# Vector products whose rows come out on their own partitions, and 32x32 transpositions for the way to columns

## The chip, the core and the metric

The kernel runs on one core of one Trainium2 chip. The metric is the device time of one execution in microseconds. Each kernel is run several times and the median is compared.

Engines are called as the profile calls them: PE (TensorE; PEld is its weight load), DVE (VectorE), ACT (ScalarE), POOL (GpSimd) and SP (SyncE). PE reads SBUF and writes PSUM. DVE and ACT read and write both.

## What is computed

One token passes through four layers, A B A B, and then back. A is attention with one query over the last 4096 positions of a cache, B is an MLP. Both A layers share their weights, and so do both B layers. The results are the output and the gradients of the input, of both caches and of all weights.

```
x = x + A(layernorm(x));  x = x + B(layernorm(x))      # twice
A(x):  q = x @ wq (1024 -> 32 heads x 128, 4 kv heads)
       p = softmax(q k^T * 128**-0.5) over the last 4096 of 32768 positions
       return (p v) @ wo                               # 4096 -> 1024
B(x):  h = x @ w1 + b1                                 # 1024 -> 3584
       return (h * tanh(softplus(h))) @ w2             # 3584 -> 1024
out, grads = value and vjp with grad_out               # all tensors bf16
```

The gradient of a cache is zero outside the last 4096 positions, so 56 MB of zeros are written. The gradients of the weights are outer products of two vectors per layer pair.

## The kernel before

All vectors are held as columns: element 128t + p on partition p, column t (for the 3584 and 4096 long ones of the MLP and of wo, element 512c + 4p + k in column 4c + k). The order of instructions on each engine is written out by hand.

**Loads.** SP loads weights in chunks of 1 MB into a ring of eight slots (class `Ring`, L71 issues). `want` lists them in order; `pump` issues as long as a slot is free; `release` frees a slot and pumps. W1, the first MLP matrix, stays in SBUF in the tile `W1`. After the way back through layer 0's MLP its place is used anew: `ring.lend(lent)` gives three slots in it to the ring, and `ROWS`, `rt`, `rf`, `RT` and `TWIN` lie in the rest of it.

**Zeros.** `zeros(n)` takes n of 56 jobs of 1 MB each and issues them on POOL from the zeroed tile `zt` (L272). The calls are spread over the program by hand, most of them behind a value that has to be there first (L267, `pz`). `zt` holds a weight chunk until POOL zeroes it in `last_da` (L808).

**Products forward.** Where a matrix is used in its natural layout, a product with a vector has two forms.

- The column form makes a 128x128 block the weights and one column the moving operand, so each block costs a weight load and a matmul of one column, and the result is a column at once. Layer 0's MLP uses it: L680 for the first product, `mlp_out` (L744) for the second, into `y_ps`. So does `dn_b0`, the way back through layer 0's first MLP product, over blocks `STAY` to 27 of W1 (`mv`, L500, into `TP`). By then these blocks have been turned in place, and only the first `STAY` = 4 blocks of each row are in natural layout; for them DVE computes eight dot products (`rowdot`, L458, into `dnp`).
- The row form (`row_mm`, L351) repeats the vector over 32 weight columns and streams the matrix, so the result is a row in PSUM, on 32 partitions alike. Four such matmuls stand side by side in four column groups of the array (`tile_position=(0, 32 * j)`).

The row form is used for layer 1's wo product and second MLP product (`rows_by_two`: even rows into groups 0 and 1, odd rows into groups 2 and 3, two halves of 512) and for layer 1's first MLP product (seven pieces of 512 in the banks `SC[0]` and `SC[1]`). The way from the rows to columns goes over DVE or ACT copies to SBUF and fp32 matmuls with the selection matrices `sel2` or `sel4` (L365 and L367 in `two_to_cols`, L689 and L692 in `mlp_fwd`). `residual` (L416) adds the old x; L705 adds the bias.

**The way back.** `rows_chunk` goes through a chunk's four rows of blocks: the first `nr` of them as dot products on DVE, the others turned by PE (`turn_pe`, L481), copied to SBUF by DVE or ACT (`evac`, L313 and L316, by a running estimate of both loads) and then multiplied in the column form (L500). `later` holds these products back a few units, and a chunk is released behind its last product. `do1`, `dp1`, `dq1` and `dn1` are hooks that are called after each chunk of the last attention's way back. `do1(4)` turns the output y to columns and adds x3.

**Rows for the outer products.** The weight gradients need the vectors as rows. `put_by` writes four of them to DRAM early on (L826) and `take_back` (L830) brings them into `ROWS`; `rowize` (L1025, L1028, L1030) and `rowize_f` (L868, L870, L872) turn others by PE, copy them by ACT and move them into `ROWS` by SP's queue. All are called within `dn_b0`, after its rows 2 and 4, besides `rowize(GA)` in `do1(0)` and `rowize(DQC)` in `dq1`.

**The end.** After g0 PE computes the outer products (L1066, L1117), DVE and ACT copy them to SBUF, and SP stores them.

Of the kernel before, what the change touches and what calls it, by code (L numbers as in the profile page):

```python
# [93 lines left out]
def kernel(  # L94
# [97 lines left out]
    nc.vector.memset(spread[:], 0.0)  # L192
    sel4 = sb([P, 4], FP32, "sel4")
    nc.vector.memset(sel4[:], 0.0)
    sel2 = sb([P, 2], FP32, "sel2")
    nc.vector.memset(sel2[:], 0.0)
    for j in range(4):
        nc.vector.memset(sel4[32 * j:32 * j + 1, j:j + 1], 1.0)
        nc.vector.memset(sel2[32 * j:32 * j + 1, j % 2:j % 2 + 1], 1.0)
    quarter = sb([P, 4], FP32, "quarter")  # L200
# [147 lines left out]

    def row_mm(bank, j, stat, mov, first, last):

        nc.tensor.matmul(bank[32 * j:32 * j + 32, :], lhsT=stat.to_broadcast([P, 32]), rhs=mov, start=first, stop=last,  # L351
                         skip_group_check=True, tile_position=(0, 32 * j))

    def rows_by_two(bank, ch, c, n, vec):

        for tt in range(4):
            k = 4 * c + tt
            for s in range(2):
                row_mm(bank, 2 * (k % 2) + s, vec(k), ch[:, tt, 512 * s:512 * s + 512], k < 2, k >= n - 2)

    def two_to_cols(bank, buf, out):

        ov = out.rearrange("p (s i) -> p i s", s=2)
        for h in range(2):
            nc.vector.tensor_copy(buf[:, 256 * h:256 * h + 256], bank[:, 256 * h:256 * h + 256])  # L365
            for i in (2 * h, 2 * h + 1):
                nc.tensor.matmul(ov[:, i, :], lhsT=buf[:, i * P:(i + 1) * P], rhs=sel2[:], start=True, stop=True,  # L367
                                 skip_group_check=True)

# [51 lines left out]

    def ln_bwd(part, n32, rstd, g, name, beside=None):

        st = tmp([P, 2], FP32, "bst")
        dn = tmp([P, TD], FP32, "dn")
        t2 = tmp([P, TD], FP32, "t2")
        if part is None:
            nc.vector.tensor_scalar(out=dn[:], in0=TP[:, 0:TD], scalar1=1.0, scalar2=0.0, op0=ALU.mult, op1=ALU.add,
                                    accum_out=st[:, 0:1])
        else:  # L430
            nc.vector.scalar_tensor_tensor(out=dn[:], in0=TP[:, 0:TD], scalar=1.0, in1=part[:], op0=ALU.mult, op1=ALU.add,
                                           accum_out=st[:, 0:1])
        nc.vector.scalar_tensor_tensor(out=t2[:], in0=dn[:], scalar=1.0, in1=n32[:], op0=ALU.mult, op1=ALU.mult,
                                       accum_out=st[:, 1:2])
        if beside is not None:
            beside(0)
        nc.tensor.matmul(TP[:, 128:130], lhsT=onesD[:], rhs=st[:], start=True, stop=True)
        if beside is not None:
            beside(1)
        ab = tmp([P, 2], FP32, "ab")  # L440
        nc.vector.tensor_copy(ab[:], TP[:, 128:130])
        nc.vector.scalar_tensor_tensor(out=t2[:], in0=n32[:], scalar=ab[:, 1:2], in1=dn[:], op0=ALU.mult,
                                       op1=ALU.subtract)
        nc.vector.tensor_scalar(out=t2[:], in0=t2[:], scalar1=ab[:, 0:1], scalar2=rstd[:, 0:1], op0=ALU.add,
                                op1=ALU.mult)
        gn = sb([P, TD], FP32, f"g_{name}")
        nc.vector.tensor_sub(gn[:], g[:], t2[:])
        return gn
# [82 lines left out]
    def attn_fwd(l, x, st, first, wo_hook, q_hook=None):  # L531
# [88 lines left out]
        for c in range(8):  # L620
            ch = ring.get(("o", l, c))
            if not first:
                rows_by_two(YR, ch, c, HQ, lambda h: OC[:, h, l:l + 1])
                wo_hook(c)
                continue
            for tt in range(4):
                h = 4 * c + tt
                for dd in range(TD):
                    nc.tensor.matmul(y_ps[:, dd:dd + 1], lhsT=ch[:, tt, dd * P:(dd + 1) * P], rhs=OC[:, h, l:l + 1],
                                     start=(h == 0 and dd == 0), stop=(h == HQ - 1), skip_group_check=True)  # L630
            ring.release(("o", l, c))
            wo_hook(c)
        if not first:
            two_to_cols(YR, small, y_ps)
        xn, stn = residual(y_ps, x, name)
# [36 lines left out]
    def mlp_fwd(l, x, st, mid):  # L672
# [9 lines left out]
        else:  # L682
            for t in range(TD):
                for c in range(7):
                    row_mm(SC[c // 4], c % 4, NB[:, t, l:l + 1], W1[:, t, 512 * c:512 * c + 512], t == 0, t == TD - 1)
            hv = [h_ps[:, 0:16].rearrange("p (j k) -> p k j", k=4), h_ps[:, 16:28].rearrange("p (j k) -> p k j", k=4)]
            for b, (buf, copy) in enumerate(((small, nc.vector.tensor_copy), (mlp_t, nc.scalar.copy))):
                n = 32 * (4, 3)[b]
                copy(buf[0:n, :], SC[b][0:n, :])  # L689
                bv = buf[0:n, :].rearrange("p (m k) -> p k m", k=4)  # L690
                for k in range(4):
                    nc.tensor.matmul(hv[b][:, k, :], lhsT=bv[:, k, :], rhs=sel4[0:n, 0:n // 32], start=True, stop=True,  # L692
                                     skip_group_check=True)

# [9 lines left out]
        V = nc.vector  # L704
        V.tensor_tensor(out=h[:], in0=h_ps, in1=b1c[:], op=ALU.add)  # L705

# [31 lines left out]
        return dict(n32=n32, rstd=rstd, deriv=deriv, act_late=act_late)  # L738

    def mlp_out(l, ch, c, y_ps):  # L740
        for tt in range(4):
            fb = 4 * c + tt
            for dd in range(TD):
                nc.tensor.matmul(y_ps[:, dd:dd + 1], lhsT=ch[:, tt, dd * P:(dd + 1) * P], rhs=AC[:, fb, l:l + 1],  # L744
                                 start=(fb == 0 and dd == 0), stop=(fb == TF - 1), skip_group_check=True)


# [42 lines left out]
    mp0 = sB0["deriv"]()  # L790
    y_ps = MV[:, 256:256 + TD]
    for c in range(7):
        mlp_out(0, ring.get(("2", 0, c)), c, y_ps)
        if c == 4:
            da_dots(c)
        if c < 5:
            ring.release(("2", 0, c))
    x2, st2 = residual(y_ps, x1, "B0")

    def last_da(k):  # L800
# [6 lines left out]
        if k:  # L807
            nc.gpsimd.memset(zt[:], 0.0)  # L808

    def wo_hook1(c):  # L810
# [17 lines left out]
    def take_back(name, base, off):  # L828
        r = DR[name][:].rearrange("(n l) p -> l n p", l=2)
        nc.sync.dma_start(ROWS[base:base + 2, off:off + r.shape[1] * P].rearrange("l (n p) -> l n p", p=P), r)  # L830

# [31 lines left out]
    def rowize_f():  # L863
# [7 lines left out]
        for l in range(2):  # L871
            nc.sync.dma_start(ROWS[64 + l:65 + l, NOFF:NOFF + F].rearrange("o (c j) -> o c j", j=512),  # L872
                              rf[:, 512 * l:512 * l + 512])
# [10 lines left out]
    def dn_b0(g):  # L884
        bcast(lambda c: DHC[:, c, 0:1], STAY)
        mv_open()
        for t in range(TD):
            rowdot(W1[:, t, 0:STAY * P], [LB[0][:, 0:512]], 512, dnp[:, t:t + 1], True)
            mv(W1[:, t, STAY * P:], TF - STAY, TP[:, t:t + 1], lambda i: DHC[:, STAY + i, 0:1], True)
            if t == 2:  # L890
                rowize(GB, TD, 96, 0)
                take_back("AC", 96, NOFF)
                take_back("NB", 64, 0)
                take_back("OC", 32, NOFF)
                take_back("NA", 0, 0)
            if t == 4:
                rowize_f()
        return ln_bwd(dnp, sB0["n32"], sB0["rstd"], g, "B0", lambda k: turn_ahead(("o", 3, 0), ((0,), (1, 2))[k]))

# [122 lines left out]
    def rowize(cols, n, base, off):  # L1022
# [6 lines left out]
        for l in range(2):  # L1029
            nc.sync.dma_start(ROWS[base + l:base + l + 1, off:off + n * P].rearrange("o (t p) -> o t p", p=P),  # L1030
                              rt[l:2 * n:2, k, :])
# [112 lines left out]
    da0 = tmp([P, HQ], FP32, "da")  # L1144
    y_ps = MV[:, 384:384 + TD]
    mv_open()
    even()
    bigs.append(SC[1])
    for c in range(7):
        ch = ring.get(("2", 1, c))  # L1150
        rows_by_two(YR, ch, c, TF, lambda fb: AC[:, fb, 1:2])
        flush()
# [11 lines left out]
    g1 = dn_b0(g2)  # L1164
    ring.lend(lent)
    nc.vector.tensor_copy(GA[:, :, 0], g1[:])
# [10 lines left out]
    def do1(c):  # L1177
        if c == 0:
            rowize(GA, TD, 32, 0)
        if c == 3:  # L1180
            todo[1].append(units_rows(32, HQ, out_5))
        if c == 4:
            two_to_cols(YR, RT.rearrange("p a t s -> p (a t s)")[:, 0:1024].bitcast(FP32), y_ps)
            nc.vector.tensor_tensor(out=x4[:], in0=y_ps, in1=x3[:], op=ALU.add)
        if c == 5:
# [29 lines left out]
    g0 = attn_bwd(0, sA0, g1, ("o", 3), ("q", 3), (), dict(do=do1, dp=dp1, dq=dq1, dn=dn1), units_a0)  # L1215
    zeros(3, g0)
    g0b = sb([P, TD], BF16, "g0b")
# [48 lines left out]
```

## Time and profile before

| | |
|---|---|
| runs | 456.04, 454.98, 455.77 us; median 455.77 |
| profiled execution | 455.47 us, span 453.7 us from first to last instruction |
| busy: PE, DVE, ACT, POOL | 327.4, 261.9, 211.4, 38.7 us |
| TensorE clock, mean granted | 0.661 |
| bytes moved | 181.41 MB: 121.84 on the queue of SP, 58.72 on that of POOL |

Busy time of an engine is not the kernel's bound by itself: the stages have different limits. PE's ends are modelled, since matmuls are pipelined. "DMA share" is the mean busy share of the 16 transfer engines, and GB/s what they moved.

### The profile page before, as it was taken

The numbers are of one execution on the slowest core, as the hardware profiler recorded it, in microseconds if no ns is written. First come the engines' busy times: TensorE is split into PE (matmuls) and PEld (weight loads), VectorE is DVE, ScalarE is ACT, GpSimd is POOL, SyncE is SP. The second block draws the span as 40 slices with busy tenths as digits, with TensorE's granted clock in tenths as the row PEclk, the third lists the DMA queues.
The fourth block names the chain that finished last, engine by engine and source line by source line (L and its number), as shares of the span: only waits on it lengthen the run. The fifth ranks groups of instructions, "written<-read, shape, count | busy, mean of one in ns | idle before, by whom it ended". The sixth has DMA issues, their size and how long they took to land. (4 is left out here: it accounts for less than half of the span.)

```text
span 453.7 us, 13076 instructions
## 1 busy us (share of the span) xinstructions
PE 327.4 (72%) x5793; PEld 251.3 (55%) x5793; DVE 261.9 (58%) x523; ACT 211.4 (47%) x246; POOL 38.7 (9%) x86
## 2 busy tenths in 40 slices
PE   3845542556599987998898778888987898889600
PEld 3735542456475686887797547887872222225300
DVE  4504746377451264377366756575386999898600
ACT  2501101011048275577066552364249999999600
POOL 1000000002123121200300101012221000000000
PEclk9955555555559879599679955788585555555555
DMA  8999999989989999999999999999999999999996
GB/s 333 422 423 417 420 418 420 416 313 423 418 363 397 406 407 408 409 392 417 423 422 420 363 387 355 359 411 395 423 413 417 413 416 421 416 422 414 406 408 268
DMA packets 28086, 181.41 MB, mean 400 GB/s; under 512 B 3674, under 2 KB 3702, under 8 KB 9462
## 3 DMA queue, kind: packets, MB, share of 16 engines
q1 hardware_dynamic: 19874, 121.84, 66.2%
q0 software_dynamic: 8064, 58.72, 31.7%
q8 instruction: 45, 0.74, 0.6%
q14 instruction: 11, 0.09, 0.1%
q10 hardware_dynamic: 92, 0.02, 0.0%
HBM read 81.84 MB, written 98.62 MB: 398 GB/s over the span
## 5 line engine op out<-in xcount | busy, mean ns | idle before, releaser
L316 ACT COPY ring<-BIG 128x1024 bf16<-128x1024 bf16 x51 | 50.5, 1015 | 43.6 <-PE BIG L481 21.6
L1066 PE MATMUL wide<-W 2*128 2x512 bf16 x228 | 52.2, 598 | 9.2 <-ACT W L316 2.0
L481 PE MATMUL BIG<-ident_bf,ring 128*128 128x128 bf16 x664 | 55.4, 238 | 3.1 <-issue 1.9
L481 PEld LDWEIGHTS <-ring 128*128 128x128 bf16 x768 | 53.3, 110 | 4.1 <-issue 3.6
L458 DVE CUSTOM_DVE_ANT_0 junk<-ring,SC 128x1024 bf16<-128x1024 bf16 x32 | 38.9, 1215 | 6.3 <-DMA ring<-in_B_w_dram 5.8
L500 PEld LDWEIGHTS <-ring 128*128 128x128 bf16 x864 | 29.6, 97 | 13.5 <-ACT ring L316 6.7
L1066 PEld LDWEIGHTS <-W 2*128 2x128 bf16 x240 | 12.5, 102 | 44.4 <-issue 43.3
L313 DVE CAST ring<-wide 128x1024 bf16<-128x1024 f32 (+1 forms) x29 | 33.8, 1201 | 3.1 <-PE wide L1066 1.1
L316 ACT CAST ring<-wide 128x1024 bf16<-128x1024 f32 (+1 forms) x35 | 32.9, 1011 | 1.3 <-PE wide L1117 0.5
L316 ACT COPY KT<-BIG 128x1024 bf16<-128x1024 bf16 x22 | 21.7, 1013 | 22.8 <-PE BIG L659 20.5
L313 DVE COPY ring<-BIG 128x1024 bf16<-128x1024 bf16 x32 | 21.8, 689 | 17.3 <-PE BIG L481 13.3
L272 POOL DMA_DIRECT2D out_dram<-zt x56 | 29.7, 534 | 21.6 <-DMA out_dram<-zt 20.8
L458 DVE CUSTOM_DVE_ANT_0 junk<-ring,DSX 128x1024 bf16<-128x1024 bf16 x24 | 29.4, 1224 | 0.8
L481 PE MATMUL BIG<-ident_bf,W 128*128 128x128 bf16 x288 | 24.6, 235 | 2.9 <-issue 2.9
L316 ACT COPY W<-BIG 128x1024 bf16<-128x1024 bf16 x21 | 20.8, 1014 | 11.2 <-PE BIG L481 10.7
L543 PE MATMUL MV<-NA,ring 128*128 128x1 bf16 x512 | 15.0, 165 | 13.1 <-DMA ring<-in_A_wq_dram 11.7
L543 PEld LDWEIGHTS <-ring 128*128 128x128 bf16 x512 | 14.6, 103 | 13.8 <-DMA ring<-in_A_wq_dram 12.4
L313 DVE CAST VS<-wide 128x1024 bf16<-128x1024 f32 (+1 forms) x17 | 19.7, 1188 | 3.6 <-PE wide L1066 3.0
L1117 PE MATMUL wide<-W 32*128 32x256 bf16 x128 | 20.9, 402 | 0.9 <-ACT ring L316 0.8
L316 ACT CAST KT<-wide 128x1024 bf16<-128x1024 f32 x20 | 20.4, 1033 | 1.8 <-PE wide L1066 0.9
L481 PEld LDWEIGHTS <-W 128*128 128x128 bf16 x288 | 19.4, 115 | 3.3 <-issue 3.3
L500 PEld LDWEIGHTS <-W 128*128 128x128 bf16 x480 | 16.6, 101 | 3.6 <-issue 2.2
(280 smaller groups left out, 537.9 us busy)
## 6 DMA issues: line engine op xcount, KB each, us to landing
out_dram<-zt POOLq DMA_DIRECT2D x56, 1024.0 KB, 14.3
ring<-in_A_wq_dram SPq DMA_DIRECT2D x24, 1024.0 KB
ring<-in_A_wo_dram SPq DMA_DIRECT2D x14, 1024.0 KB
ring<-in_B_w_dram SPq DMA_DIRECT2D x13, 1024.0 KB
W<-in_A_wo_dram SPq DMA_DIRECT2D x10, 1024.0 KB
W<-in_B_w_dram SPq DMA_DIRECT2D x8, 896.0 KB
out_dram<-ring SPq DMA_DIRECT2D x7, 1024.0 KB
out_dram<-ring SPq DMA_DIRECT2D x13, 512.0 KB
```

The costliest lines, as they stand in the source:

```text
L272: nc.gpsimd.dma_start(dst, zt[:])
L313: nc.vector.tensor_copy(dst, src)
L316: nc.scalar.copy(dst, src)
L458: nc.vector.tensor_tensor_reduce(out=out, in0=a, in1=vec, scale=1.0, scalar=acc if i else 0.0, op0=ALU.mult, op1=ALU.add, accum_out=acc)
L481: nc.tensor.transpose(b[:, i * P:(i + 1) * P], block(w, i) if block else w[:, i * P:(i + 1) * P], ident_bf[:])
L500: nc.tensor.matmul(out, lhsT=w[:, i * P:(i + 1) * P], rhs=rhs_of(i), start=fresh[0], stop=last and i == n - 1, skip_group_check=True)
L543: nc.tensor.matmul(q_ps[:, h:h + 1], lhsT=ch[:, h * P:(h + 1) * P], rhs=NA[:, t, l:l + 1], start=(k == 0 and h == 0), stop=(k == TD - 1), ...
L1066: nc.tensor.matmul(b[:, 512 * i:512 * i + 512], lhsT=R[at:at + 2, lo:lo + P], rhs=R[at:at + 2, ro + 512 * i:ro + 512 * i + 512], start=Tru ...
L1117: nc.tensor.matmul(b[:, k * 256:(k + 1) * 256], lhsT=RT[32 * g:32 * g + 32, a, tp, :], rhs=YS[32 * g:32 * g + 32, :], start=True, stop=Tru ...
```

## The change

1. `rows_by_two` becomes `out_rows`. For each row of blocks, group j now computes those 256 outputs that belong on its own 32 partitions: of each of the eight 128-blocks the elements 32j to 32j + 31. All groups use the same vector column. `two_to_cols` becomes `to_eight`: one DVE transposition of 32x32 blocks over 128x256, whose first column in each block is the column form. The consumer reads it from SBUF with a stride of 32.
2. Layer 1's first MLP product does the same, with 512 columns a group in `SC[0]` and 384 in `SC[1]`; two transpositions and two bias additions follow.
3. Layer 0's second MLP product uses `out_rows` in place of `mlp_out`.
4. `dn_b0` uses the row form over blocks 4 to 27, into `SC[1]`. The eight dot products run in reverse order, and `ring.lend(lent)` comes ahead of `ln_bwd` instead of behind it.
5. `rowize(GB)`, the four `take_back` and `rowize_f` move from `dn_b0` into `do1`, at chunks 0, 1 and 2. All row moves of `rowize`, `rowize_f` and `take_back` are issued by ACT instead of SP.
6. One zero job moves from behind g0 to behind the zeroing of `zt`.
7. `sel2` and `sel4` and their ten memsets go.

```diff
-    def rows_by_two(bank, ch, c, n, vec):
+    def row_mms(bank, n, vec, mov, first, last):
+        for j in range(4):
+            m = mov(j)
+            nc.tensor.matmul(bank[32 * j:32 * j + 32, 0:n].rearrange("p (g a) -> p g a", a=m.shape[-1]),
+                             lhsT=vec.to_broadcast([P, 32]), rhs=m, start=first, stop=last, skip_group_check=True,
+                             tile_position=(0, 32 * j))
+    def out_rows(ch, c, n, vec):
         for tt in range(4):
             k = 4 * c + tt
-            for s in range(2):
-                row_mm(bank, 2 * (k % 2) + s, vec(k), ch[:, tt, 512 * s:512 * s + 512], k < 2, k >= n - 2)
+            row_mms(YR, 256, vec(k), lambda j: ch[:, tt, :].rearrange("p (g q a) -> p q g a", q=4, a=32)[:, j],
+                    k == 0, k == n - 1)
+    def to_eight(bank, buf):
+        nc.vector.transpose(buf[:, 0:256], bank[:, 0:256])
+        return buf[:, 0:256].rearrange("p (g m) -> p g m", m=32)[:, :, 0]
...
             for t in range(TD):
-                for c in range(7):
-                    row_mm(SC[c // 4], c % 4, NB[:, t, l:l + 1], W1[:, t, 512 * c:512 * c + 512], t == 0, t == TD - 1)
+                for b, (c0, c1) in enumerate(((0, 4), (4, 7))):
+                    row_mms(SC[b], 128 * (c1 - c0), NB[:, t, l:l + 1],
+                            lambda j: W1[:, t, :].rearrange("p (c q x) -> p q c x", q=4, x=P)[:, j, c0:c1],
+                            t == 0, t == TD - 1)
...
+            parts = ((0, small, 0, 16), (1, mlp_t, 16, 12))
+            for b, buf, f0, n in parts:
+                V.transpose(buf[:, 0:32 * n].rearrange("p (c k m) -> p c k m", k=4, m=32),
+                            SC[b][:, 0:32 * n].rearrange("p (c a k) -> p c k a", k=4, a=32))
+            for b, buf, f0, n in reversed(parts):
+                V.tensor_tensor(out=h[:, f0:f0 + n], in0=buf[:, 0:32 * n].rearrange("p (f m) -> p f m", m=32)[:, :, 0],
+                                in1=b1c[:, f0:f0 + n], op=ALU.add)
...
-        mlp_out(0, ring.get(("2", 0, c)), c, y_ps)
+        out_rows(ring.get(("2", 0, c)), c, TF, lambda fb: AC[:, fb, 0:1])
...
-        nc.sync.dma_start(ROWS[base:base + 2, off:off + r.shape[1] * P].rearrange("l (n p) -> l n p", p=P), r)
+        nc.scalar.dma_start(ROWS[base:base + 2, off:off + r.shape[1] * P].rearrange("l (n p) -> l n p", p=P), r)
...
     def dn_b0(g):
-        for t in range(TD):
+        for fb in range(STAY, TF):
+            row_mms(SC[1], 256, DHC[:, fb, 0:1], lambda j: W1[:, :, fb * P + 32 * j:fb * P + 32 * j + 32],
+                    fb == STAY, fb == TF - 1)
+        for t in reversed(range(TD)):
             rowdot(W1[:, t, 0:STAY * P], [LB[0][:, 0:512]], 512, dnp[:, t:t + 1], True)
-            mv(W1[:, t, STAY * P:], TF - STAY, TP[:, t:t + 1], lambda i: DHC[:, STAY + i, 0:1], True)
-            if t == 2: rowize(GB, TD, 96, 0); take_back(...)   # four of them
-            if t == 4: rowize_f()
+        ring.lend(lent)
...
     def do1(c):
         if c == 0:
             rowize(GA, TD, 32, 0)
+            rowize(GB, TD, 96, 0)
+        if c == 1: take_back(...)                              # the four
+        if c == 2: rowize_f()
         if c == 4:
-            two_to_cols(YR, RT.rearrange("p a t s -> p (a t s)")[:, 0:1024].bitcast(FP32), y_ps)
+            y = to_eight(YR, RT.rearrange("p a t s -> p (a t s)")[:, 0:512].bitcast(FP32))
```

## Prediction

> **What bounds the kernel now.** I read the page's slices first, because no engine is full: PE, the busiest, has 72% of the span. The transfer rows look different.
>
> ```profile
> DMA  8999999989989999999999999999999999999996
> GB/s 333 422 423 417 420 418 420 416 313 423 418 363 397 406 407 408 409 392 417 423 422 420 363 387 355 359 411 395 423 413 417 413 416 421 416 422 414 406 408 268
> DMA packets 28086, 181.41 MB, mean 400 GB/s; under 512 B 3674, under 2 KB 3702, under 8 KB 9462
> ```
>
> Nearly every slice moves 405 to 423 GB/s. All 181.41 MB at 420 would take 432 us of the 453.7. So the time is bytes over rate, plus what the transfers lose in a few dips. I then cut the trace at each dip, and at the end (columns: stretch, length, the engines' busy time, TensorE's clock, DMA share, GB/s).
>
> ```profile
> 94.50:98.50 4.00, 3.17 (x119) 3.16 (x119) 3.68 (x15) 0.61 (x1) 0.00 (x0) 0.50 0.48 129
> 132.50:135.00 2.50, 2.18 (x33) 0.71 (x33) 1.49 (x4) 0.96 (x1) 1.86 (x4) 0.50 0.34 138
> 198.00:201.00 3.00, 3.00 (x71) 2.91 (x68) 2.33 (x5) 2.87 (x4) 0.00 (x0) 1.00 1.00 322
> 254.50:258.00 3.50, 2.64 (x56) 1.87 (x53) 3.29 (x6) 2.12 (x3) 0.70 (x2) 1.00 0.78 265
> 267.00:270.00 3.00, 2.53 (x35) 1.69 (x35) 2.41 (x4) 0.82 (x2) 0.00 (x0) 0.50 0.96 303
> 277.50:282.00 4.50, 4.50 (x134) 4.14 (x132) 4.29 (x13) 0.37 (x2) 0.39 (x1) 0.50 0.94 253
> 286.00:290.00 4.00, 4.00 (x42) 4.00 (x39) 2.71 (x13) 1.01 (x1) 0.00 (x0) 0.55 0.75 247
> 306.00:308.00 2.00, 2.00 (x46) 1.94 (x45) 0.46 (x3) 1.56 (x3) 0.00 (x0) 0.82 0.95 283
> 341.60:428.00 86.40, 74.92 (x395) 26.52 (x393) 77.42 (x72) 81.08 (x92) 1.75 (x4) 0.50 1.01 416
> 428.00:453.70 25.70, 0.00 (x0) 0.00 (x0) 0.12 (x1) 0.00 (x0) 0.00 (x0) 0.50 0.87 346
> ```
>
> A dip of length d at rate r loses d x (1 - r/420). In order: 2.8, 1.7, 0.7, 1.3, 0.8, 1.8, 1.65, 0.65 us, 11.4 together. The last two rows are the ruler: from 341.6 transfers are full, compute ends at 428, and stores drain alone for 25 us. **So a microsecond saved by compute counts only if it closes a dip before 308.** The bytes are the same after the change.
>
> **The change, part by part.**
>
> *The second MLP's first product (layer 1).* Its end, in the timeline:
>
> ```profile
> 151.03 0.69 DVE L689 COPY junk<-SC 128x512 f32<-128x512 f32 x1 [5.03 <-PE SC L351]
> 151.24 0.58 ACT L689 COPY DSX<-SC 96x512 f32<-96x512 f32 x1 [3.54 <-PE SC L351]
> 151.77 2.03 PE L692 MATMUL MV<-sel,junk 128*128 128x4 f32 x8 [0.59 <-DVE junk L689]
> 153.66 2.01 PE L692 MATMUL MV<-sel,DSX 96*128 96x3 f32 x8
> 155.78 0.19 DVE L705 TENSOR_TENSOR DSX<-MV,b1c 128x28 f32<-128x28 f32 x1 [4.06 <-PE MV L692]
> ```
>
> From the rows in PSUM to the bias add it takes 155.78 - 151.03 = 4.75 us, 4 of them fp32 selections on PE. After, VectorE transposes 512 and 384 columns and adds twice. No transposition is in this trace. Lower bound: the 512-column copy's 0.69, so 0.69 + 0.55 = 1.25. Upper bound: twice that, 2.5. I take 1.3, because L562's reduction reads the same bank at a stride of 64 values, and costs 0.69 too. With 0.1 more until both adds have been issued, 3.3 us go (2.1 at the upper bound). The Trainium skill speaks against it: "SBUF — State Buffer", section Door 1, gives PSUM 8-byte lines and says that non-contiguous patterns slow matmuls there much. Carried over to VectorE, which the L562 row denies, it would mean the upper bound. Its page "VectorE: DVE Perf Modes", section The three transpose paths, gives 311 ns for a 128x128 bf16 transposition; an estimate from that is 2.2 us for the two, and 0.9 us less gain. The product streams 512 + 384 instead of 1024 column times in each of 8 steps (a bank's four column groups run side by side; the second bank's had only three): 12% of 5.16 us, 0.6 us.
>
> *Layer 1's wo product.* Two copies, eight fp32 selections and the wait until L416 run from 142.11 to 143.68, 1.57 us. One 256-column transposition takes 0.42 (L365's copy), so 1.1 us go. 128 matmuls of 256 columns stand for 64 of 512: the same columns, at four groups. A pair of load and matmul can follow the last in 0.022 us (16 pairs of L377 in 0.34), while four groups of 256 columns need 0.107 a row at full clock (half of 256 x 0.83 ns, next paragraph), 0.027 a pair, so I take nothing; the bound is 0.034 a pair (L500, 16 in 0.54), 0.1 us a chunk, 0.8 in all.
>
> *Layer 0's second product.* At half clock L351 starts four 512-column matmuls every 0.43 us (its loads at 146.76, 147.19, 147.61), 0.83 ns a column time. 32 pairs a chunk take 0.88 us (160 in 4.41); 4 x 256 column times take 0.85. So the first release, which ends the dip at 94.5, moves by 0.1 either way. Transposing adds 0.4 to 0.8 ahead of L416, but the q product stands 1.28 us waiting for its seventh chunk at 112.44; that covers it. Without the cover it would cost its length.
>
> *One zero store moves* from after g0 to behind POOL's memset of zt (111.09 + 3.51). It is issued at 114.6; POOL's next piece, the QC copy at 116.4, stays clear of its 0.53. It shares the channel with wo loads, which end some 2.4 us later, at 135. Their last chunk is used at 141. The dip at 132.5 goes: 1.6 us.
>
> *What the 5 us of earlier compute buy up to 276.* Zero stores fill 136 to 198 at 405 GB/s, so nothing is gained there; but the next loads are asked for 4 to 5 us earlier, while zeros are still queued. The dips at 198 and 254.5 then fill: 1.6 of their 2.0. The one at 267 comes from chunks loaded one release at a time; it stays.
>
> *Back through layer 0's first matrix (dn_b0).* 192 pairs, broken by two detours and a stall of 1.9 us, end at 285.9. After: 24 x 256 x 0.83 ns at half clock, 5.1 us, from 277.2 to 282.3; the eight row dots end at 283.3, as now; a transposition of 0.42: 283.8. g comes 2.1 us earlier. The three lent loads need only the products and rows 5 to 7, so they can go at 282.4, not 287.34:
>
> ```profile
> 283.19 4.05 SPq L872 DMA_DIRECT2D W<-W  x2
> 287.34 2.69 SPq L71 DMA_DIRECT2D W<-in_A_wo_dram  x3
> 305.12 0.30 ACTq L333 DMA_DIRECT2D out_dram<-W  x1
> ```
>
> *What ACT gets.* Ten row transfers are now issued by ACT between its copies in the next stage: 10 x 0.30 = 3.0 us, plus copies of 0.25 and 1.0. That stage runs at 2.15 us a chunk, of which ACT's two copies take 1.93. Worse, a transfer waits for the previous user of its completion semaphore. By the two builds' order, the third take_back stands behind the last lent load. From 284.4 about 1.1 MB of zeros and 3.1 MB of loads are due, so that load lands at 294.4. ACT arrives at about 293: 1.2 us more. Behind it stand the copies that PE needs for its banks. In all 5.5 us, less 1.9 of gaps that ACT has there now (1.04 ahead of its copy at 292.41, the rest in slivers of 0.2): 3.6 us.
>
> *The output's columns at chunk 4.* In this stage the same selections block PE:
>
> ```profile
> 300.51 0.74 DVE L365 COPY W<-YR 128x256 f32<-128x256 f32 x2
> 300.98 1.05 PE L367 MATMUL MV<-sel,W 128*128 128x2 f32 x8 [0.94 <-DVE W L365]
> 302.54 1.93 ACT L316 COPY W<-BIG 128x1024 bf16<-128x1024 bf16 x2 [2.27 <-PE BIG L481]
> ```
>
> Row dots of chunks 4 and 5 start 4.29 us apart instead of 2.15. With 0.42 for the transposition, 1.7 go. So from 276 to 308: -2.1 + 3.6 - 1.7 = -0.2, and I take -0.5, since some of ACT's issue will overlap. The dips there (1.8, 1.65, 0.65) move more than they shrink.
>
> **Sum.** 1.6 + 1.6 + 0.5 = 3.7 us off the profiled 455.47 (span 453.7 and 1.77 around it) is 451.8. The median of the runs is 0.3 higher, 455.77; I stay with 451.8. Its own range is 450.3 to 453.5: the upper bounds cost 1.2 (transposition) and 0.5 (pairs), and the dip at 267 plus ACT's waits are worth 1.5 the other way.
>
> **Rivals.** *More closes:* ACT's issues hide, and the lent loads fill 286 too. Then 1.5 to 3.2 of the 4.9 us of dips that are left after 132 close as well: 450.3 to 448.6. For: 286 is a pure lack of requests. Against: ACT has 0.2 us free a chunk. 0.18.
>
> *Only the zero store counts:* earlier compute just waits for loads, since transfers are already full from 202 to 254. 455.5 - 1.6 = 453.9, up to 454.8. 0.10. *Nothing:* new dips open where old ones close: 455.5. 0.09.
>
> *ACT becomes the bound (slower).* If its issues cost what SP's did (1.43 and 4.05 for pairs, 1.52 for four: 7.0 us) and the lent load lands as late as 297, ACT owes 7.0 + 1.25 + 4 - 1.9 = 10.4 instead of 3.6. The stage is then 6.8 longer, and 451.8 becomes 458.6. It decides from 3.7 us beyond my 3.6. Against: ACT's own two issues cost 0.30 and 0.29. 0.10. *The change does not do what it says:* with pieces of 32 elements, the column groups run one after another. dn_b0 alone then takes 4 x 5.1 = 20.4 us instead of 5.1: over 465. L351's groups overlap now, though with contiguous columns. 0.03.
>
> **Numbers.** 0.2% is 0.9 us, about what a measurement here can tell from no change. Faster: 0.50 + 0.18 + 0.10 = 0.78; same 0.09; slower 0.13. The range 448.6 to 455.6 leaves out the slower cases and a few below.
>
> **What would show it.** Right: the bias add 1.3 us after the second MLP's product; no dip at 132; none at 198 and 254; lent loads issued near 282; ACT waiting at its take_back in the next stage. Wrong: transpositions above 1.2 us for 512 columns; matmuls of one row not overlapping; ACT's issues far from 0.30; dips of the same sum elsewhere; or a compute end within some us of the last store, so that transfers were no longer the end.

## The result: slower by 0.3%, and the profile after

The changed kernel takes 456.91 us (median of 8 runs, 456.37 to 457.35) against 455.44 us before (8 runs, 454.03 to 456.04): ratio 1.0033, 95% interval 1.0020 to 1.0047. The forecast was 451.8 us, range 448.6 to 455.6. The profiled execution took 457.25 us, 1.78 us more than the one of before.

The page of the changed kernel, the same rows as before:

```profile
DMA  8999999979999999999999999859999999999997
GB/s 335 422 421 419 418 420 420 419 312 425 395 422 419 422 418 414 398 417 420 424 422 423 423 417 382 328 181 371 419 392 405 408 416 419 415 420 416 406 408 298
DMA packets 28085, 181.40 MB, mean 398 GB/s; under 512 B 3674, under 2 KB 3702, under 8 KB 9462
```

The bytes are the same. The dip of 363 in the twelfth slice is gone, the one of 363 and 387 in the 23rd and 24th too, and in their place the 27th slice moves 181. The trace cut at the old dips, and at the new one (columns as before: stretch, length, busy time of PE, PEld, DVE, ACT and POOL, TensorE's clock, DMA share, GB/s):

```profile
132.50:135.00 2.50, 2.50 (x40) 1.63 (x36) 0.77 (x2) 0.06 (x1) 2.50 (x6) 0.50 1.01 426
198.00:201.00 3.00, 3.00 (x49) 3.00 (x48) 1.48 (x3) 1.39 (x2) 0.00 (x0) 0.66 0.99 415
254.50:258.00 3.50, 0.39 (x12) 0.30 (x13) 0.46 (x3) 1.78 (x2) 0.00 (x0) 1.00 1.00 419
267.00:270.00 3.00, 2.40 (x42) 1.92 (x42) 2.27 (x3) 0.15 (x1) 0.00 (x0) 0.50 0.98 410
277.50:282.00 4.50, 3.19 (x58) 2.41 (x50) 3.61 (x17) 0.35 (x1) 0.00 (x0) 0.88 1.00 415
286.00:290.00 4.00, 2.70 (x64) 2.63 (x64) 2.44 (x4) 1.27 (x2) 0.00 (x0) 1.00 1.00 418
294.00:304.00 10.00, 6.08 (x92) 5.81 (x92) 1.83 (x3) 5.38 (x6) 0.00 (x0) 0.50 0.35 121
433.00:455.50 22.50, 0.00 (x0) 0.00 (x0) 0.00 (x1) 0.00 (x0) 0.00 (x0) 0.50 0.88 351
```

Six of the dips shown before, which moved 138, 322, 265, 303, 253 and 247 GB/s, now move 410 to 426; the first, at 94.5, stays (127 GB/s). All the more was to be gained, and one hole takes it away: 121 GB/s over 10 us. The timeline shows what stood still there (columns: start, length, engine, line, what; in brackets the idle time before it and what ended that):

```profile
278.95 2.11 SPq L71 DMA_DIRECT2D W<-in_A_wo_dram  x3
...
291.32 0.26 ACTq L819 DMA_DIRECT2D W<-dr_AC  x1
293.82 0.25 ACTq L819 DMA_DIRECT2D W<-dr_NB  x1
294.11 0.28 ACTq L819 DMA_DIRECT2D W<-dr_OC  x1
296.29 0.23 ACTq L819 DMA_DIRECT2D W<-dr_NA  x1
296.61 1.93 ACT L309 COPY ring<-BIG 128x1024 bf16<-128x1024 bf16 x2 [7.08 <-DMA W<-in_A_wo_dram]
297.68 1.01 PE L857 MATMUL BIG<-ident_bf,DHC 128*7 128x128 bf16 x8 [6.67 <-ACT ring L309]
```

L819 is `take_back`. Its four transfers, 4 to 16 KB each, don't leave one after the other: they leave at 291.3, 293.8, 294.1 and 296.3, while ACT does nothing else for 7.08 us. What ends the wait is a lent load of 1 MB, in which `take_back` has no part. PE waits 6.67 us for ACT's copy, no chunk is released, and SP issues the next three wq loads from 300.12 (296.22 before). From 294 to 302 the transfers that are left move 90 GB/s and less.

The trace shows why ACT waits. A transfer reports that it has landed to a completion semaphore, in sixteen counts. In the built program the transfers of SP and ACT take eight such semaphores in turn, and `dr_AC`, `dr_NB` and `dr_NA` get those that the three lent loads had before. The last counts of these loads come at 291.30, 293.80 and 296.26; the three `take_back`s leave at 291.32, 293.82 and 296.29. The last count is also late by itself: the eighth count of the third lent load comes at 291.10, the sixteenth 5.2 us later.

To compare the kernels I add up what the transfers lost: for each stretch its length, less its bytes at 416 GB/s (the rate of the prediction's full stretch), from the trace cut every 0.5 us, up to the last piece in which something moves. A figure below 0 means a rate above 416. All figures are us, each of one profiled execution.

| kernel (its experiment) | profiled time | median | 0 to 140 | 140 to 292 | 292 to 346 | 346 to 440 | from 440 | lost in all |
|---|---|---|---|---|---|---|---|---|
| before | 455.47 | 455.44 | 5.9 | 6.8 | 0.6 | 0.2 | 2.9 | 16.4 |
| changed | 457.25 | 456.91 | 4.5 | 0.6 | 10.4 | 0.6 | 1.9 | 18.0 |
| rows by POOL (2) | 452.94 | 452.71 | 4.8 | 0.3 | 0.8 | 1.6 | 6.0 | 13.5 |
| the same, zero store back (8) | 452.14 | 452.08 | 4.3 | 1.4 | 0.3 | 0.8 | 6.1 | 12.9 |
| only take_back by ACT (9) | 451.84 | 451.69 | 4.5 | -1.0 | 2.4 | 0.8 | 6.2 | 13.0 |
| (8) with a later zero store (10) | 453.83 | 453.52 | 4.2 | 5.3 | 1.5 | 0.3 | 3.2 | 14.5 |

The losses of the change: 1.4 + 6.2 us less up to 292, 9.8 more from 292 to 346, 0.4 more after that, and 1.0 less at the end: 1.6 us more, of the 1.78 by which the two profiled executions differ.

### The profile page after: what moved, and what is told of

Its sections match the earlier page's. It is cut to its first block, busy times and chain, and to the rows that moved or that the text cites. A ratio compares the mean times of both kernels' runs of the same rounds, so it can differ in the third digit from the quotient of the medians.

```text
span 455.5 us, 12838 instructions
## 1 busy us (share of the span) xinstructions
PE 318.3 (70%) x5681; PEld 244.4 (54%) x5681; DVE 262.0 (58%) x515; ACT 210.6 (46%) x245; POOL 38.9 (9%) x86
## 5 line engine op out<-in xcount | busy, mean ns | idle before, releaser
L474 PE MATMUL BIG<-ident_bf,ring 128*128 128x128 bf16 x664 | 55.2, 237 | 3.6 <-ACT W L1013 1.6
L474 PEld LDWEIGHTS <-ring 128*128 128x128 bf16 x768 | 52.8, 109 | 5.3 <-issue 4.8
L493 PEld LDWEIGHTS <-ring 128*128 128x128 bf16 x864 | 30.5, 98 | 10.4 <-issue 6.5
L474 PE MATMUL BIG<-ident_bf,W 128*128 128x128 bf16 x288 | 25.7, 243 | 2.0 <-issue 1.7
L474 PEld LDWEIGHTS <-W 128*128 128x128 bf16 x288 | 20.3, 117 | 2.2 <-issue 2.1
L347 PE MATMUL YR<-ring,AC 128*32 128x256 bf16 x208 | 10.9, 368 | 11.0 <-DMA ring<-in_B_w_dram 8.6
```

The source lines that it names most:

```text
L347: nc.tensor.matmul(bank[32 * j:32 * j + 32, 0:n].rearrange("p (g a) -> p g a", a=m.shape[-1]), lhsT=vec.to_broadcast([P, 32]), rhs=m, star ...
L474: nc.tensor.transpose(b[:, i * P:(i + 1) * P], block(w, i) if block else w[:, i * P:(i + 1) * P], ident_bf[:])
L493: nc.tensor.matmul(out, lhsT=w[:, i * P:(i + 1) * P], rhs=rhs_of(i), start=fresh[0], stop=last and i == n - 1, skip_group_check=True)
```

## The experiments

**Theory W:** Three of ACT's four `take_back`s get completion semaphores that the lent loads still hold. ACT stands until those have landed, chunk copies stand behind it, and loads are not asked for. **Rivals:** ACT is simply too busy with issues; the new row forms, or the earlier compute, are worth less than was thought.

**1. The four take_backs and rowize_f moved from chunks 1 and 2 of that stage to chunk 5, still on ACT.**

```
-        if c == 1:
+        if c == 5:
             take_back("AC", 96, NOFF)
             ...
-        if c == 2:
             rowize_f()
```

> The changed kernel, with the four take_back and rowize_f called at chunk 5 of the last attention's way back instead of at chunks 1 and 2. ACT still issues all of them in the same stage, but by the build's order they no longer wait for a semaphore that a lent load holds. Theory W (ACT's queue stands still behind a transfer whose completion semaphore is still held by a lent load, 7.1 us): the stall goes, the hole in the transfers at 294 to 304 goes, and the time falls by 5 to 8 us to 449 to 452. Rival I (ACT has too many issues and copies in this stage, whatever they wait for): the work is the same, so at most 1.5 us are gained, 455.5 or more.

Measured: 459.48 us, ratio 1.0080 (1.0064 to 1.0097), slower still. The wait moved along. ACT's timeline at the new place:

```profile
299.68 0.29 ACTq L819 DMA_DIRECT2D W<-dr_AC  x1
...
304.36 1.09 ACTq L819 DMA_DIRECT2D W<-dr_NA  x1
305.63 1.00 ACT L859 COPY W<-BIG 7x1024 bf16<-7x1024 bf16 x1 [6.32 <-DMA W<-dr_NA]
...
312.54 1.93 ACT L309 COPY W<-BIG 128x1024 bf16<-128x1024 bf16 x2 [5.90 <-DMA W<-W]
```

From 290 to 298 the stage runs a chunk each 2.14 us with no wait of ACT. Then it waits twice, 6.3 and 5.9 us. By the counts of the semaphores, `dr_OC` leaves when the first wq load has landed (301.50), `dr_NA` when a small store that ACT itself issued at 298.40 has (304.34), and the first transfer of rowize_f when another wq load has (310.91). So my expectation of 449 to 452 was wrong: what matters is not only the lent loads, but whichever transfer had the next semaphore, and here each of these was still in flight.

**2. All row moves at the same places, issued by POOL.**

```
-            nc.scalar.dma_start(ROWS[...
+            nc.gpsimd.dma_start(ROWS[...      (three lines: rowize, take_back, rowize_f)
```

> The changed kernel, with all row transfers of rowize, rowize_f and take_back issued by POOL's queue at the same places of the program; POOL has its own completion semaphores, and nothing else to do in this stage. ACT keeps its two small copies. Theory W: as for the later take_back, 449 to 452. Rival I: the issue cost leaves ACT (3 us), so 453 to 455. A third theory, C (the rows are late because the transfer engines are full, whoever asks): the rows come late again, but nobody waits for them before chunk 7; it would not tell itself from W here by time, but the rows would land 10 us or more after their issue.

Measured: 452.71 us, ratio 0.9934 (0.9919 to 0.9949). ACT waits for no load, and the loss from 292 to 346 falls from 10.4 to 0.8 us. Everything else of the change is in this kernel, so the rest of it is a gain.

**3. Row moves ahead of the lent loads, on ACT, in dn_b0.**

```
     def dn_b0(g):
         ...
+        rowize(GB, TD, 96, 0)
+        take_back("AC", 96, NOFF)      (and the other three)
+        rowize_f()
         ring.lend(lent)
```

> The changed kernel, with rowize(GB), the four take_back and rowize_f put in dn_b0 ahead of the lending, still issued by ACT, which stands idle there for 9.6 us. Theory W: they now wait for semaphores of the four loads before the lent ones, which were issued from 259 to 273 and land by about 285; ACT may stand until 285 instead of starting its copies at 281.6, so some 3 us of the 7 come back as a stall: 451 to 454. Rival I: the issues leave the crowded stage, so the time falls by 3 to 4 us, 453. What tells them apart is whether ACT's wait is seen on the loads of wo.

Measured: 456.90 us, ratio 1.0028 (1.0013 to 1.0043): no gain over the change. ACT's timeline:

```profile
280.98 0.25 ACTq L819 DMA_DIRECT2D W<-dr_NB  x1
285.99 0.23 ACTq L819 DMA_DIRECT2D W<-dr_OC  x1
290.90 0.23 ACTq L819 DMA_DIRECT2D W<-dr_NA  x1
291.18 1.00 ACT L859 COPY W<-BIG 7x1024 bf16<-7x1024 bf16 x1 [13.54 <-DMA W<-in_A_wo_dram]
```

Three issues of 0.25 us stand 5.0 and 4.9 us apart, and ACT is idle for 13.54 us in all. 1 MB in 5 us is half of 416 GB/s, the pace of loads that share the transfers with zero stores. In the built program `dr_NB` and `dr_OC` get semaphores of the loads ahead of the lent ones, whose last counts come at 280.96 and 285.96, and `dr_NA` still gets that of the first lent load (290.88). Put ahead of the lent loads, the row moves mostly wait for older loads instead.

**4. Before the change, the zero store alone moved.**

```
             nc.gpsimd.memset(zt[:], 0.0)
+            zeros(1)
     ...
-    zeros(3, g0)
+    zeros(2, g0)
```

> The kernel before, with only the one zero store moved from behind g0 to behind the zeroing of zt. The prediction's price: the dip at 132.5 closes, 1.6 us less, ratio 0.9965. Rival: wo's loads are held up by as much as the dip gives, and the ratio is 1.000.

Measured: 454.04 us, ratio 0.9965 (0.9951 to 0.9980), 1.5 us less against the 1.6 of the prediction.

**5. Before the change, the row moves alone.** The second rowize, the four take_backs and rowize_f go from dn_b0 to the next stage and from SP to ACT.

```
     def dn_b0(g):
         ...
-                rowize(GB, TD, 96, 0)
-                take_back(...)                 (and rowize_f)
     def do1(c):
         if c == 0:
             rowize(GA, TD, 32, 0)
+            rowize(GB, TD, 96, 0)
+        if c == 1:
+            take_back(...)                     (c == 2: rowize_f)
-    nc.sync.dma_start(ROWS[...
+    nc.scalar.dma_start(ROWS[...
```

> The kernel before with one thing of the change alone: the row moves (second rowize, the four take_backs, rowize_f) are issued by ACT in the stage of do1 instead of by SP in dn_b0. Theory W (ACT's take_backs wait for lent loads to land, and transfers then run dry): ACT stands 4 to 9 us at a take_back, transfers drop under 100 GB/s for several us between 294 and 306, and the whole takes what separates the changed kernel from the version whose rows go by POOL, 4.2 us more: 459 to 460, ratio 1.007 to 1.010. Rival (the wait bites only because the changed kernel's ACT arrives 6 us earlier there): no wait over 2 us, 455.0 to 456.5.

Measured: 459.52 us, ratio 1.0079 (1.0053 to 1.0106), the number of theory W. This part alone costs 4.5 us.

```profile
279.66 3.83 SPq L71 DMA_DIRECT2D W<-in_A_wo_dram  x3
...
294.94 1.93 ACT L316 COPY ring<-BIG 128x1024 bf16<-128x1024 bf16 x2 [2.50 <-DMA W<-in_A_wo_dram]
...
298.41 6.00 SPq L71 DMA_DIRECT2D ring<-in_A_wq_dram  x3
```

The wait of ACT behind the lent load is only 2.5 us here, less than W said: ACT arrives at 292.4 instead of 289.5, and the last lent load has landed at 294.60 instead of 296.26. On the length of the wait the rival was nearer, on the time W. The price is higher than the wait: SP, freed of the row moves, asks for the lent loads at 279.66 instead of 287.34, they have landed by 295, one load follows at 292.47, and the wq loads only at 298.41, when a stage that is behind its time has released its chunks (296.22 before). Transfers fall to 53 GB/s between 298 and 300. How much of the 4.5 us is ACT's wait, and how much comes from the loads that go out earlier, isn't separated.

**6. The change, with the row moves back on SP in dn_b0, in its new, backward loop.**

```
-        for t in reversed(range(TD)): rowdot(...)
+        for t in reversed(range(TD)):
+            rowdot(...)
+            if t == 5: rowize(GB, TD, 96, 0); take_back(...)      (four, all row moves by nc.sync)
+            if t == 3: rowize_f()
         ring.lend(lent)
```

> The changed kernel with the row moves put back to SP in dn_b0, as before the change; all other parts stay. Theory W: no wait of ACT behind a lent load, no hole at 294; SP's issues cost the lent loads some us of their head start, so 452 to 453.5, near the version whose rows go by POOL (452.7). Rival (POOL's queue was what helped there, or the new row forms slow the stage): 455 or more.

Measured: 458.10 us, ratio 1.0054 (1.0034 to 1.0073). This one tells nothing on the theory, because of how I built it. The loop runs from the last row block to the first, and the rows' room is that of the first blocks. So rows were written there before the last two row dots, which therefore read moved rows instead of the matrix, and VectorE waited 12.44 us for the transfers. Experiment 11 is the same without this fault.

**7. Before the change, the second MLP's first product alone in the new form,** with its two transpositions.

```
-                for c in range(7):
-                    row_mm(SC[c // 4], c % 4, NB[:, t, l:l + 1], W1[...])
+                for b, (c0, c1) in enumerate(((0, 4), (4, 7))):
+                    row_mms(SC[b], 128 * (c1 - c0), NB[:, t, l:l + 1], ...)
-            (two copies, eight selections, one add)
+            (two transposes of VectorE, two adds)
```

> The kernel before with the second MLP's first product alone in the new form (four groups of 128 and 96 outputs a partition group, two 32x32 transpositions instead of two copies and sixteen selections). The prediction's step: the bias add comes 3.9 us earlier and closes part of the dips at 198 and 254.5, 1.2 us: 454.0 to 454.6. Rival (later stages just wait for their loads, which are not asked for earlier): dh0 moves under 1 us and the time stays at 455.2 to 455.9.

Measured: 455.43 us, ratio 1.0003 (0.9986 to 1.0020). dh1, which follows from the bias add, comes at 155.16 instead of 159.62, 4.5 us earlier, and nothing comes of it. 1.2 us (0.9974) lies outside the interval.

**8. Experiment 2 with the zero store put back behind g0.**

```
             nc.gpsimd.memset(zt[:], 0.0)
-            zeros(1)
     ...
-    zeros(2, g0)
+    zeros(3, g0)
```

> The version whose rows go by POOL, with the zero store put back behind g0. If the zero store's 1.6 us and the rest add up: 454.2 to 454.6 (452.7 + 1.6), dip at 132 there again. Rival (that version's end is set by one lagging DMA engine, which works through at 25 GB/s for its last 6 us while the others are idle, so that a dip of the others costs nothing): 452.4 to 453.2, with a shorter tail.

Measured: 452.08 us, ratio 0.9931 (0.9904 to 0.9957). The zero store, worth 1.5 us alone, shows no worth here (0.9931 without the move, 0.9934 with it): the dip at 132 hardly returns (389 GB/s from 132 to 134, 381 from 136 to 138), since the wo loads are asked for earlier. And the end looks as the rival said:

```profile
443.00:446.00 3.00, 0.00 (x0) 0.00 (x0) 0.00 (x0) 0.00 (x0) 0.00 (x0) 0.50 0.07 27
446.00:449.00 3.00, 0.00 (x0) 0.00 (x0) 0.00 (x0) 0.00 (x0) 0.00 (x0) 0.50 0.06 25
```

A DMA share of 0.06 is one engine of sixteen. One works for 6 us while fifteen have nothing left.

**9. The change, with rowize and rowize_f by POOL, and the four take_backs left on ACT at their place.**

```
 rowize:     -   nc.scalar.dma_start(ROWS[base + l:...      + nc.gpsimd.dma_start(
 rowize_f:   -   nc.scalar.dma_start(ROWS[64 + l:...        + nc.gpsimd.dma_start(
 take_back:      nc.scalar.dma_start(ROWS[base:base + 2,...   (unchanged)
```

> The changed kernel with rowize and rowize_f issued by POOL, and the four take_backs left where they are, on ACT. The built program then gives the take_backs completion semaphores that older, landed loads hold (none of the three lent loads'). Theory W (ACT stands still because its take_backs get the semaphores of lent loads in flight): the four take_backs issue at 290 to 292 without a wait over 0.5 us, no hole at 294 to 304, and the time is that of the version whose rows all go by POOL, 452.2 to 453.2. Rival (any issue by ACT in that stage holds up its copies, whatever the semaphore): a wait of some us at the take_backs remains, 454.5 or more.

Measured: 451.69 us, ratio 0.9914 (0.9890 to 0.9937), the lowest median of all. Its timeline:

```profile
283.40 0.26 ACTq L819 DMA_DIRECT2D W<-dr_AC  x1
283.69 0.33 ACTq L819 DMA_DIRECT2D W<-dr_NB  x1
284.06 0.28 ACTq L819 DMA_DIRECT2D W<-dr_OC  x1
284.92 0.23 ACTq L819 DMA_DIRECT2D W<-dr_NA  x1
...
290.15 5.04 SPq L71 DMA_DIRECT2D ring<-in_A_wq_dram  x3
```

The same four transfers, on the same engine, at the same place of the program, leave within 1.75 us instead of 5.2. They leave 8 us earlier than in the changed kernel, while the lent loads (issued at 275.70) are still in flight: PE waits for one of them until 290.12 and for another until 294.34. The wq loads are asked for at 290.15, not 300.12. Of these 8 to 10 us, 3.2 are there before the edit can act: the changed kernel's profiled execution issues the lent loads at 278.95. Experiment 2, which issues them at 278.54, asks for the wq loads at 291.18. What differs by the edit is which completion semaphores the take_backs get: SP's and ACT's transfers share eight in this program, in turn, POOL's have others, and with four row transfers fewer in the turn the take_backs fall on semaphores of loads issued ahead of the lent ones. Three of these landed at 279.72 or earlier; the fourth, that of `dr_NA`, gets its last count at 284.90, and `dr_NA` leaves at 284.92. The two pairs of issues that ACT was spared (1.79 and 1.29 us in the changed kernel) are a part of the earlier start; that part isn't separated from the rest.

**10. Experiment 8, with one more zero store moved from behind dh1 (151 us) to behind g0.**

```
-    zeros(8, dh1)
+    zeros(7, dh1)
     ...
-    zeros(3, g0)
+    zeros(4, g0)
```

> The version whose rows go by POOL, with the zero store behind g0 as before the change, and one more 1 MB zero store moved from the group behind dh1 (151 us) to behind g0. Bytes are the same. 1 MB takes 2.5 us at 414 GB/s. Theory L (one DMA engine has more to do than the other fifteen and works on while they are idle; the 6 us tail at 25 GB/s is what is left of it, so a dip of the others is filled by it): the loss ahead of 200 grows by 1.5 to 2.5 us, the tail shrinks by about as much, and the time stays within 0.8 us of 452.1. Rival (a dip costs its length): 454.0 to 454.6, tail unchanged.

Measured: 453.52 us, ratio 0.9959 (0.9943 to 0.9975), 1.4 us more than experiment 8, between the two expectations; the intervals of the two ratios overlap (0.9943 to 0.9957), so this difference is not quite clear of the noise. The dip opened elsewhere than I said. From 262 to 284, experiment 8 and then this one:

```profile
262.00:284.00 22.00, 14.94 (x252) 12.07 (x248) 13.32 (x42) 6.18 (x8) 1.81 (x5) 0.71 1.01 406
```

```profile
262.00:284.00 22.00, 16.11 (x256) 12.30 (x256) 14.30 (x42) 4.99 (x6) 1.25 (x3) 0.63 0.91 334
```

By the table, the loss from 140 to 292 grew by 3.9 us, and from 440 on it shrank by 2.9. So in these two executions a dip costs part of its length, not all of it. The sixteen counts of the last zero store fit the shorter tail: the last of them comes 4.0 us after the eighth here, 10.7 us in experiment 8. But near 297 us the same figure is 1.0 here and 0.7 there, so it isn't shown that the dip at 262 is what shortened the tail.

**11. The change, with the row moves on SP in dn_b0 and the row dots in the old order.**

```
-        for t in reversed(range(TD)): rowdot(...)
+        for t in range(TD):
+            rowdot(...)
+            if t == 2: rowize(GB, TD, 96, 0); take_back(...)      (four, all row moves by nc.sync)
+            if t == 4: rowize_f()
         ring.lend(lent)
```

> The changed kernel with the row moves on SP inside dn_b0, at the places of the kernel before, and dn_b0's row dots in its old order so that the rows' room is free. The lent loads then go behind the row moves and the last row dot, near 287 instead of 279. Theory W: no wait of ACT behind a lent load and no hole at 294 to 304, but dips of 2 to 4 us between 278 and 292 as in the kernel before: 452.5 to 454.5. Rival (only POOL's queue makes the gain): 455 or more.

Measured: 452.02 us (11 runs, 451.63 to 454.43), ratio 0.9943 (0.9921 to 0.9964). As W expected (0.5 us below its range), there is no wait of ACT behind a load, and no hole from 294 to 304; in its profiled execution (454.27 us) SP issues the lent loads only at 289.40, and transfers fall to 20 to 142 GB/s from 284 to 290. So it isn't POOL's queue that makes the gain: three ways to keep ACT from waiting, by POOL, by other semaphores, by SP, end with medians within 1.1 us of each other.

## Why the prediction was wrong, step by step

**The step that failed is "What ACT gets".** It had the mechanism by name (a transfer waits for the previous user of its completion semaphore; that it is the fourth take_back that stands behind the last lent load, not the third, and that two others stand behind the other two, changes little), and mis-sized it: 1.2 us of wait, 3.6 us in all, where the profile shows 7.08 us of wait and a loss from 292 to 346 that is 9.8 us larger. Three numbers went into it. The landing was nearly right: 294.4 was said, 296.3 is when it lands and the last take_back leaves. ACT's arrival was not: 293 was said, and ACT ended its copy at 289.5, in part because dn_b0's transposition ended at 280.29 instead of 283.8. What I got wrong most is what the wait costs. I took ACT's lost time as the price. But no chunk is released meanwhile, and so the loads behind it are not asked for: the wq loads of 300.12 stand where those of 291.18 stand in experiment 2, whose lent loads go out within 0.5 us of the changed kernel's, and from 294 the transfers had little to move. Experiments 2, 9 and 11 take the wait away in three ways, and each is faster than before by 0.6 to 0.9%; experiment 5 puts the row moves alone into the kernel before, and it loses 4.5 us with a shorter wait.

The rival "ACT becomes the bound" had this place, the late landing (297 against 296.3) and the sign, with a chance of 0.10 and 458.6 us. Its price for issues was half right: the single ones took 0.23 to 0.28 us, the pairs 1.79 and 1.29, close to SP's 1.43.

**The second MLP's product** gave more than was said. The profile's rows after, from the transpositions on:

```profile
146.94 0.72 DVE L697 STREAM_TRANSPOSE junk<-SC 128x512 f32<-128x512 f32 x1 [2.96 <-PE SC L347]
147.58 0.54 DVE L697 STREAM_TRANSPOSE DSX<-SC 128x384 f32<-128x384 f32 x1
...
148.37 0.18 DVE L701 TENSOR_TENSOR DSX<-junk,b1c 128x16 f32<-128x16 f32 x1
```

1.26 us for the two transpositions, against 1.3 forecast at the lower bound; 1.43 from the rows to the second add, against 4.75 before, which is the 3.3 us. The reading at a stride of four values costs hardly more than a copy (0.72 against 0.69 for 512). What the Trainium skill's page "SBUF — State Buffer", section Door 1, says of matmuls would, carried over to VectorE, have had it slower, and the estimate of 2.2 us worked out from its page "VectorE: DVE Perf Modes", section The three transpose paths, was too much: the trace agrees with neither. The product itself took 3.10 us (143.84 to 146.94) instead of 5.16, a gain of 2.1 where 0.6 was said, since its clock was 1.00 in that stretch, against 0.67 before.

**The other compute steps** held or gave more: x3 comes 2.0 us earlier (1.1 forecast for its own step), dn_b0's product runs from 273.79 to 278.90, 5.1 us (5.1 forecast, so its four groups do run side by side), the 256-column transposition 0.45 (0.42), the lent loads at 278.95 (282.4 forecast). dh1 came 7.5 us earlier, dh0 only 3.6: in between, the loads set the pace.

**"What the 5 us of earlier compute buy" and the zero store** were added up as if dips were independent. Each dip from 132 to 290 did close, that at 267 too, which was to stay. But experiment 7 shows 4.5 us of earlier compute worth nothing alone, and experiments 2 and 8 show no worth of the zero store beside the rest, though it is worth 1.5 us alone (experiment 4). With the wait gone (experiment 9) the table has 9.2 us less loss up to 292 than before, of which 3.3 come back after 440, 1.8 from 292 to 346 and 0.6 from there to 440. So the 451.7 us of experiment 9 lie on the forecast of 451.8 by luck, not by its sum: more closed than the 3.7 us of it, and a part was given back at the end. The step "a microsecond saved by compute counts only if it closes a dip" needs the addition that even a closed dip need not count.

## What to carry to other kernels

Before a small transfer is moved onto an engine that also computes, list in the built program which completion semaphore it gets, who had it last, and whether that transfer has landed by then; a wait is priced by the loads that are not asked for meanwhile, not by the engine's lost time. If stages ahead get faster, the engine arrives earlier while the load lands no earlier, and a short wait turns into a long one (2.5 us in experiment 5, 7.08 in the changed kernel). Where the last microseconds show a DMA share near one sixteenth, take the sum of closed dips as an upper bound of the gain, not the gain: in experiment 9, 9.2 us less loss up to 292 became 3.6 us.

## What the runs showed of the hardware that was not expected

- A transfer that takes 0.26 us to issue held ACT for about 2 us at a time in the changed kernel and for nearly 5 in experiment 3, although SP had issued the load that it waited for. The Trainium skill's page "DMA: Bandwidth & Descriptors", section Issuing engines are not separate DMA queues, says that issuing from several engines only saves the sequencer's issue time. Here the engine that issues the other row moves decided 5 us, one way (ACT, changed kernel, 456.91) or the other (POOL, experiment 9, 451.69), because it decided which semaphores were shared.
- The stall cost PE its clock. In the changed kernel eight transpositions of L474 take 0.61 us at 290.23, and 1.01 us from 298.62 to 304.77 after 6.67 us without work; the clock is 1.00 from 291 to 292, 0.61 from 292 to 293 and 0.50 from 294 to 304. The Trainium skill's "TensorE: Matmul & The Clock Gate", section HAM oscillation, says that idle gaps over 3.4 us bring this about. The gap of 6.67 us agrees with that, but the clock falls within the second microsecond after PE's last work at 291.0, before 3.4 us have passed. It lengthened six groups of eight transpositions by 0.4 us each, after the wait was over.
- A part of each transfer ends late: 25 to 27 GB/s for 6 us at the end of experiments 2, 8 and 9, while before the tail was 3 us and with the hole of the changed kernel 2 us. The sixteen counts of each zero store show it earlier. At 153 us the last count comes 0.8 to 1.8 us after the eighth in these kernels and in experiment 10. While transfers stay full this grows, to 10.9 us at 280 in the changed kernel and to 10.6 at 272 in experiment 9, but only to 6.0 at 254.5 before, where dips lie between. Then it falls in all of them, with a hole or without, to 0.4 to 1.4 us between 296 and 321. At the last zero store (356 to 359 us) it is 10 to 11 us in experiments 2, 8 and 9, but 2.3 in the changed kernel, 3.5 before and 4.0 in experiment 10, and the tail follows it. A late part also makes a load report its landing later: the last counts of the lent loads came 5.2 to 5.5 us after the eighth in the changed kernel, 1.5 to 1.6 us in experiment 5. Which engine this is, whether it is always the same one, and why it falls behind in some kernels more than in others, is open.
